# First maxima ahead of VectorE's tables, weights ahead of the last stores, two banks for a pair: five small edits to a fused attention, expert and gated-product kernel

## The chip, the cores and the metric

One Trainium2 chip, one core. The metric is device microseconds of the whole kernel, the median of repeated runs. An engine's queue runs its instructions in the order in which they were issued, and the kernel's author sets that order. SyncE (SP) and ScalarE (ACT) issue transfers on queues of their own, GpSimd (POOL) on a third.

## The reference

```python
# 1. attention with 32 global tokens and a window: B=4, H=8, 512 local + 32 global rows, D=64
k_all, v_all = concatenate([k_g, k_l], axis=2), concatenate([v_g, v_l], axis=2)
out_g = matmul(sm(scale * matmul(q_g, k_all.T)), v_all)            # global rows see everything
s_ll = where(abs(i - j) <= 32, scale * matmul(q_l, k_l.T), -1e9)   # local rows see a band
a_l = sm(concatenate([scale * matmul(q_l, k_g.T), s_ll], axis=-1)) # and the global rows
out_l = matmul(a_l, v_all)
x = rows of concatenate([out_g, out_l], axis=2)                    # 2304 tokens x 512
# 2. top-1 mixture of 8 experts, tokens with x @ w_skip <= 0 pass through
e_idx = argmax(xc @ w_gate, axis=1); gate_w = softmax(xc @ w_gate)[e_idx]
y[e_idx == e] = gate_w * (maximum(xc[e_idx == e] @ w1[e], 0) @ w2[e])   # w1[e] 512 x 1024
out = x; out[do_compute] = xc + y
# 3. gated product
return ((out @ w_a) * (out @ w_b)) @ w_out                         # 512 x 1536, 1536 x 512
```

## The kernel before, in words

Three phases follow each other in one program, 0 to about 132 us, to about 276 us, and to the end.

**Attention.** It runs over 16 pairs of heads (`NPAIR`), four pairs to a batch. For a pair p, `emit_S` makes the scores in PSUM (L963, half a pair per call with k), `emit_M` adds the band mask and takes row maxima on VectorE (L975), `emit_E` does the exponentials on ScalarE (L986) and, on GpSimd, copies the columns of the global keys to a tile of their own (`smg`, L988). `emit_T` transposes both (L1000, L1010). `emit_PV` multiplies with the values (L1026 and L1035) into a PSUM tile `o` of two banks and copies it to `ot` on ScalarE (L1040). `emit_X` multiplies `ot` with a table `xi` (L1059), which holds an identity to turn the rows and the router's weights beside it, so that VectorE then reads both router scores `lg` (L1063) and tokens `xt` (L1073) from the same `o` banks. The pool `ps_o` of these banks is shared by consecutive pairs; the pool `ps_s` holds six single banks for scores and transposes. The two pairs at the end (`last_pairs`) are written out by hand; `NPAIR - 2` is the last but one.

Each pair is cut into four slots (slot = 4 x pair and up), and side work hangs on slot numbers: `ROUTES` (routing of a batch), `SCATTERS` (the slots at which GpSimd scatters the four 128-row tiles of a batch to the experts' regions `xs`, L1252), and `GSTEPS` (the global queries' passes). `ZEROS` says in which pair SP stores which of the 16 blocks of zero rows to `xs` (L927, from the tile `zrow`); the scatters wait until these have landed. All loads and stores of a pair are put in a list `pend` and issued by SP one after the other. `start()` builds the table `xi`, issues its loads, runs the first two pairs' scores, maxima and exponentials, and keeps TensorE busy with matmuls that compute nothing (`idle`, L1371).

**Experts.** `WORK` lists the pieces (expert, first tile, number of row tiles); each is worked off in four quarter steps. One step is 12 matmuls of the first layer (L243), transposes (L1502) and six of the second (L1516), with weights that SP loads as `raw` (`fetch`, L152), ScalarE rounds to `hi` (L171) and VectorE subtracts to `lo` (L181). `st.fetch(i)` issues the loads of step i, two of 512 KB. `st.store_last()` issues the four stores of the last batch's tokens (L1264, x2d<-xt); `load_rows(2)` loads rows of work 2 (L157), which wait for the scatters. A scatter of the finished rows (L1528) waits for the stores of the last batch.

**Gated product.** `Late` runs 18 row tiles through `w_a`, `w_b` (L527) and `w_out` (L557), with sums kept in DRAM. The last tile is added in two halves of 256 columns (L559), each stored by its own DMA (L560).

## Time and profile before

| | us |
|---|---|
| median of three runs | 697.33 |
| lowest, highest | 695.45, 699.65 |
| the profiled execution's own time | 698.71 |
| its span in the profile | 696.9 |

The span runs from the first to the last event that the profiler records on the core; the time of the execution is 1.8 us longer. The profile gives busy time per engine, windows with the granted TensorE clock (1.00 is full speed) and the DMA engines' share, a timeline with the idle time before each piece of work and what released it, and a chain of work followed back from the end. "issue" in brackets means that the profile shows nothing that the engine waited for. SPq and ACTq are rows of the instruction queues that issue transfers; a row's length there includes waiting.

### The profile page before, as it was taken

What the parts mean: (1) busy time and instruction counts of PE and PEld (TensorE: products, weight loads), DVE (VectorE), ACT (ScalarE), POOL (GpSimd) and SP (SyncE); (2) the same over time, 40 slices, a digit from 0 to 9 for tenths busy, and PEclk for the clock granted to TensorE, in tenths of its full rate; (3) what the DMA queues carried; (4) which work ended last, traced back from release to release, by engine and by line L of the source; (5) the groups of instructions that cost most, each with busy time, mean ns of one, the idle gap of its engine ahead of it and who ended that gap; (6) DMA issues with size and microseconds to landing.
All of it is one profiled execution on the core that took longest, in us unless ns stands there. A gap on an engine that the chain in (4) does not pass through costs nothing.

```text
span 696.9 us, 16731 instructions
## 1 busy us (share of the span) xinstructions
PE 674.1 (97%) x6329; PEld 604.6 (87%) x6329; DVE 490.6 (70%) x1278; ACT 397.0 (57%) x973; POOL 130.8 (19%) x213
## 2 busy tenths in 40 slices
PE   8898999989999999999999999999999999999996
PEld 5777887868998888879999999999999999999995
DVE  5667878986968999967975796856375656544444
ACT  5667778865857884567467554544454544443220
POOL 4002213130101210010111122312231232212000
PEclk9999999999999999999999999999999999999999
DMA  8898778799999936632785589996599679549853
GB/s 282 219 233 281 240 222 280 229 310 361 371 369 346 346 121 228 219 134 92 226 333 128 77 188 327 313 221 119 65 268 216 121 151 327 75 61 213 288 179 111
DMA packets 86141, 154.86 MB, mean 222 GB/s; under 512 B 8663, under 2 KB 40279, under 8 KB 84516
## 3 DMA queue, kind: packets, MB, share of 16 engines
q1 hardware_dynamic: 69236, 110.80, 49.1%
q0 software_dynamic: 15744, 42.87, 27.5%
q8 instruction: 52, 0.85, 0.5%
q14 instruction: 37, 0.30, 0.1%
q10 hardware_dynamic: 1072, 0.04, 0.1%
HBM read 105.95 MB, written 51.18 MB: 225 GB/s over the span
## 4 chain that ended last, share of the span: by engine, by line
PE 80%; ACT 3%; DMA 3%; DVE 3%; issue 1%; POOL 0%; SPq 0%; DVEq 0%; POOLq 0%
PE bank L527 32%; PE bank L557 19%; PE acc L1516 8%; PE ph L243 6%; PE bank L583 3%; DMA raw<-w 3%; PE ph L235 2%; PE o L1059 1%; PE sps L963 1%; PE bank L462 1%; PE pt L1502 1%; ACT sm L986 1%; PE o L1035 1%; PE tps L1000 1%; PE tp L204 1%
## 5 line engine op out<-in xcount | busy, mean ns | idle before, releaser
L527 PE MATMUL bank<-xh,w 128*128 128x256 f32 (+1 forms) x1232 | 251.4, 290 | 0.1
L527 PEld LDWEIGHTS bank<-xh,w 128*128 128x128 f32 x1232 | 200.5, 189 | 4.2 <-DVE tmp L649 0.4
L527 PE MATMUL bank<-xl,w 128*128 128x256 f32 (+1 forms) x616 | 178.4, 290 | 0.0
L557 PE MATMUL bank<-woh,g 128*128 128x512 f32 (+1 forms) x412 | 143.7, 392 | 1.2 <-ACT o L563 0.5
L527 PEld LDWEIGHTS bank<-xl,w 128*128 128x128 f32 x616 | 116.1, 188 | 4.2
L181 DVE TENSOR_TENSOR lo<-raw,hi 128x1024 fp32r<-128x1024 f32 x72 | 87.0, 1221 | 11.9 <-ACT hi L171 10.8
L557 PEld LDWEIGHTS bank<-woh,g 128*128 128x128 f32 x412 | 77.3, 188 | 15.6 <-ACT o L563 1.0
L557 PE MATMUL bank<-wol,g 128*128 128x512 f32 (+1 forms) x206 | 80.4, 390 | 0.0
L171 ACT ACTIVATE hi<-raw 128x1024 fp32r<-128x1024 f32 x72 | 75.4, 1054 | 7.8 <-PE acc L1516 4.4
L607 ACT ACTIVATE g<-tmp 128x256 fp32r<-128x256 f32 (+1 forms) x88 | 37.8, 431 | 69.7 <-DVE tmp L649 68.9
L564 POOL DMA_DIRECT2D out<-raw x48 | 39.1, 815 | 141.6 <-ACT raw L563 127.0
L639 DVE TENSOR_TENSOR tmp<-bank,tmp 128x256 f32<-128x256 f32 (+1 forms) x44 | 18.8, 440 | 58.5 <-PE bank L527 58.4
L563 ACT ACTIVATE raw<-bank 128x512 f32<-128x512 f32 x48 | 28.6, 595 | 51.6 <-PE bank L557 50.5
L986 ACT ACTIVATE sm<-sm,nm 128x160 f32<-128x160 f32 x128 | 52.9, 419 | 7.8 <-DVE nm L975 7.8
L564 POOL DMA_DIRECT2D out<-o x37 | 29.6, 801 | 139.2 <-ACT o L563 101.7
L607 ACT ACTIVATE tmp<-bank 128x256 f32<-128x256 f32 (+1 forms) x88 | 34.6, 400 | 25.7 <-PE bank L527 22.2
L649 DVE TENSOR_TENSOR tmp<-bank,tmp 128x256 f32<-128x256 f32 (+1 forms) x88 | 38.9, 442 | 11.7 <-PE bank L527 10.2
L557 PEld LDWEIGHTS bank<-wol,g 128*128 128x128 f32 x206 | 38.7, 188 | 4.6
L645 DVE TENSOR_TENSOR g<-tmp,g 128x256 fp32r<-128x256 f32 (+1 forms) x88 | 38.3, 437 | 3.1 <-ACT g L607 1.4
L563 ACT ACTIVATE o<-bank 128x512 f32<-128x512 f32 x37 | 21.9, 596 | 31.9 <-PE bank L557 29.9
L243 PE MATMUL ph<-hi,xh 128*128 128x256 f32 x132 | 40.0, 303 | 0.0
L243 PE MATMUL ph<-hi,xl 128*128 128x256 f32 x132 | 37.5, 284 | 0.0
(265 smaller groups left out, 1276.5 us busy)
## 6 DMA issues: line engine op xcount, KB each, us to landing
raw<-w SPq DMA_DIRECT2D x64, 512.0 KB
out<-raw POOLq DMA_DIRECT2D x48, 256.0 KB, 4.6
out<-o POOLq DMA_DIRECT2D x37, 256.0 KB, 4.5
raw<-qk SPq DMA_DIRECT2D x28, 272.0 KB
xr<-x2d SPq DMA_DIRECT2D x25, 256.0 KB
raw<-wa SPq DMA_DIRECT2D x12, 512.0 KB
raw<-wb SPq DMA_DIRECT2D x12, 512.0 KB
raw<-wo SPq DMA_DIRECT2D x12, 512.0 KB
```

The source lines that it names most:

```text
L171: nc.scalar.activation(hi, rv, AF.Copy)
L181: nc.vector.tensor_tensor(lo, rv, hi.bitcast(F32), ALU.subtract)
L243: nc.tensor.matmul(ph, lhsT=x[:, d, :], rhs=w[:, d, :], start=(z == 0), stop=(z == 11))
L527: self.nc.tensor.matmul(bank[:, 0:n], lhsT=w[:, k], rhs=x[:, xp, k], start=start and z == 0, stop=z == 5, skip_group_check=not start)
L557: nc.tensor.matmul(acc[:, c], lhsT=a, rhs=w[:, c], start=(j == 0 and z == 0), stop=(j == 1 and z == 2))
L563: nc.scalar.activation(o, acc, AF.Copy)
L564: i = nc.gpsimd.dma_start(dst, o, accum_op=ALU.add if g else ALU.bypass)
L607: cp = lambda o, i: nc.scalar.activation(o, i, AF.Copy)
L645: tt(g4[2 * j + 1][:, h], (u, p)[h][j], g4[2 * j].bitcast(F32)[:, h], ALU.subtract)
L649: tt(v, (b1, b2)[h][j][:, 0:n], v, ALU.mult)
L986: st_.exp = nc.scalar.activation(sm, sm, AF.Exp, bias=nm[:, hh, j:j + 1], scale=-1.0, accum_out=dens[p][:, k, j, hh:hh + 1]).ins
L1516: nc.tensor.matmul(acc, lhsT=a[:, j, c], rhs=w[:, j, :], start=(q == 0 and z == 0), stop=(q == NQ - 1 and z == 5))
```

## The change

Five edits. (1) In `start()`, the eight copies of `ident` into `xi` move from VectorE to ScalarE, behind its three DMA issues; the copies of `tokid` and `pb8` on VectorE move from before the attention to the end of `start()`; the second call of `idle` goes. (2) `ZEROS` spreads the zero rows over pairs 0, 1, 2, 3, 5 and 6 (4, 3, 2, 2, 3, 2 blocks, before 3, 4, 3, 4 and 2 in pairs 0, 1, 2, 3 and 5), the first batch's scatters move from slots 24, 26, 28, 30 to 28, 29, 31, 33, and one pass of the global queries from slot 49 to 51. (3) For the last pair but one, `o` is two single banks of `ps_s` instead of one tile of `ps_o`; the copies and products that read it are done bank by bank. (4) `st.fetch(7)` is called ahead of `st.store_last()`. (5) The last half of the last output tile is stored from ScalarE's queue instead of SP's.

```diff
@@ -32,13 +32,13 @@
 
 ROUTES = (18, 34, 50)
 
-SCATTERS = ((24, 26, 28, 30), (35, 39, 43, 47), (51, 51, 53, 53))
+SCATTERS = ((28, 29, 31, 33), (35, 39, 43, 47), (51, 51, 53, 53))
 
 REUSE = 2
 
 LEAD = 38
 
-ZEROS = {0: (0, 3), 1: (3, 7), 2: (7, 10), 3: (10, 14), 5: (14, 16)}
+ZEROS = {0: (0, 4), 1: (4, 7), 2: (7, 9), 3: (9, 11), 5: (11, 14), 6: (14, 16)}
 
 WORK = [(0, 0, 1), (1, 0, 1), (1, 1, 1), (3, 0, 1), (2, 0, 2), (0, 1, 1), (4, 0, 1), (5, 0, 1), (6, 0, 1), (7, 0, 1)]
 
@@ -53,7 +53,7 @@
 WRAW, RAW2 = 6, 3
 
 GSTEPS = {(0, 0): (3, 5, 6), (0, 1): (8, 13, 14), (1, 0): (16, 21, 22), (1, 1): (24, 29, 30),
-          (2, 0): (32, 37, 38), (2, 1): (40, 45, 46), (3, 0): (43, 49, 54), (3, 1): (48, 53, 57)}
+          (2, 0): (32, 37, 38), (2, 1): (40, 45, 46), (3, 0): (43, 51, 54), (3, 1): (48, 53, 57)}
 
 
 
@@ -557,7 +557,7 @@
                         nc.tensor.matmul(acc[:, c], lhsT=a, rhs=w[:, c], start=(j == 0 and z == 0), stop=(j == 1 and z == 2))
                 if g == self.NM // 2 - 1:
                     nc.vector.tensor_tensor(o[:, c], acc[:, c], o[:, c], ALU.add)
-                    nc.sync.dma_start(dst[:, c], o[:, c])
+                    (nc.scalar if c.start else nc.sync).dma_start(dst[:, c], o[:, c])
             if g < self.NM // 2 - 1:
                 o = self.o[n % len(self.o)]
                 nc.scalar.activation(o, acc, AF.Copy)
@@ -939,9 +939,6 @@
         for b in range(B):
             nc.gpsimd.iota(tokid[32 * b:32 * b + 32, NT - 1:NT], pattern=[[0, 1]], base=b * (SL + SG), channel_multiplier=1)
 
-        nc.vector.tensor_copy(xg[:, 513:514].bitcast(I32), tokid[:, 16:17])
-        nc.vector.tensor_copy(base, pb8)
-
 
         sms = [c1.tile([128, 2, 2, 2, 160], F32, name=f"sm{k}") for k in range(2)]
         smg = [c1.tile([128, 2, 2, 2, SG], F32, name=f"smg{k}") for k in range(2)]
@@ -1016,14 +1013,19 @@
 
         def emit_PV(p):
 
-            o = oxs[p] = ps_o.tile([128, 2, 512], F32, tag="o", name="o")
+            if p == NPAIR - 2:
+                both, o = None, [ps_s.tile([128, 512], F32, tag="s", name="o2") for k in range(2)]
+            else:
+                both = ps_o.tile([128, 2, 512], F32, tag="o", name="o")
+                o = [both[:, k] for k in range(2)]
+            oxs[p] = both, o
             vt = vts[p]
             for j in range(2):
                 for k in range(2):
                     r = slice(64 * k, 64 * k + 64)
                     for hh in range(2):
                         c = slice(64 * hh, 64 * hh + 64)
-                        mm = nc.tensor.matmul(o[c, k, 128 * j:128 * j + 128], lhsT=vt[r, WIN, c], rhs=pts[p, 2][r, j, :],
+                        mm = nc.tensor.matmul(o[k][c, 128 * j:128 * j + 128], lhsT=vt[r, WIN, c], rhs=pts[p, 2][r, j, :],
                                               start=(j == 0), stop=False, skip_group_check=True)
             tick(mm)
             for i in range(4):
@@ -1032,12 +1034,17 @@
                     c = slice(64 * w, 64 * w + 64)
                     for hh in range(2):
                         r = slice(64 * hh, 64 * hh + 64)
-                        mm = nc.tensor.matmul(o[r, k, 128 * j + 64 * w:128 * j + 64 * w + 64], lhsT=vt[:, 2 * i + w, r],
+                        mm = nc.tensor.matmul(o[k][r, 128 * j + 64 * w:128 * j + 64 * w + 64], lhsT=vt[:, 2 * i + w, r],
                                               rhs=pts[p, hh][:, i, c], start=False, stop=True, skip_group_check=True)
                 if i % 2:
                     tick(mm)
             ot = ots[p] = ot_p.tile([128, 2, 2, 128], F32, tag="ot", name="ot")
-            st_.ot = nc.scalar.activation(ot.rearrange("p k j q -> p k (j q)"), o[:, :, 0:256], AF.Copy).ins
+            of = ot.rearrange("p k j q -> p k (j q)")
+            if both is None:
+                for k in range(2):
+                    st_.ot = nc.scalar.activation(of[:, k], o[k][:, 0:256], AF.Copy).ins
+            else:
+                st_.ot = nc.scalar.activation(of, both[:, :, 0:256], AF.Copy).ins
 
         xt, lg, lgp = {}, {}, {}
 
@@ -1053,15 +1060,17 @@
                 xt[b] = x_p.tile([128, 4, ROW], F32, tag="xt", name="xt")
                 lg[b] = r_p.tile([128, 4, 6, 9], F32, tag="lg", name="lg")
                 lgp[b] = r_p.tile([128, 4, 3, 9], F32, tag="lgp", name="lgp")
-            o, ot = oxs.pop(p), ots.pop(p)
+            (both, o), ot = oxs.pop(p), ots.pop(p)
             for k in range(2):
                 for j in range(2):
-                    mm = nc.tensor.matmul(o[:, k, 146 * j:146 * j + 146], lhsT=ot[:, k, j, :], rhs=xi[:, hp, :], start=True, stop=True)
+                    mm = nc.tensor.matmul(o[k][:, 146 * j:146 * j + 146], lhsT=ot[:, k, j, :], rhs=xi[:, hp, :], start=True, stop=True)
             tick(mm)
-            xp = o[:, :, 0:292].rearrange("p k (j h c) -> p k j h c", j=2, h=2)
+            parts = [(slice(0, 2), both[:, :, 0:292])] if both is not None else [(slice(k, k + 1), o[k][:, None, 0:292]) for k in range(2)]
+            xps = [(k, x.rearrange("p k (j h c) -> p k j h c", j=2, h=2)) for k, x in parts]
             ld = lg[b][:, :, 2 * hp:2 * hp + 2, :] if hp < 3 else lgp[b][:, :, 1:3, :]
-            nc.vector.tensor_tensor(ld.rearrange("p (k j) h e -> p k j h e", k=2), xp[:, :, :, :, 64:73],
-                                    dens[p][:, :, :, :, None].to_broadcast([128, 2, 2, 2, 9]), ALU.mult)
+            for k, xp in xps:
+                nc.vector.tensor_tensor(ld.rearrange("p (k j) h e -> p k j h e", k=2)[:, k], xp[:, :, :, :, 64:73],
+                                        dens[p][:, k, :, :, None].to_broadcast([128, k.stop - k.start, 2, 2, 9]), ALU.mult)
             if hp == 1:
                 nc.gpsimd.tensor_copy(xt[b][:, :, 513].bitcast(I32), tokid[:, 4 * b:4 * b + 4])
 
@@ -1070,10 +1079,10 @@
                     nc.vector.tensor_reduce(lgp[b][:, :, 0, :], lg[b].rearrange("p t h e -> p t e h"), AX.X, ALU.add)
 
             def tokens():
-                nc.vector.tensor_tensor(
-                    xt[b][:, :, 128 * hp:128 * hp + 128].rearrange("p (k j) (h d) -> p k j h d", k=2, h=2),
-                    xp[:, :, :, :, 0:64],
-                    dens[p][:, :, :, :, None].to_broadcast([128, 2, 2, 2, 64]), ALU.mult)
+                xv = xt[b][:, :, 128 * hp:128 * hp + 128].rearrange("p (k j) (h d) -> p k j h d", k=2, h=2)
+                for k, xp in xps:
+                    nc.vector.tensor_tensor(xv[:, k], xp[:, :, :, :, 0:64],
+                                            dens[p][:, k, :, :, None].to_broadcast([128, k.stop - k.start, 2, 2, 64]), ALU.mult)
                 sums()
 
             return tokens
@@ -1373,15 +1382,15 @@
         def start():
             nc.vector.memset(xi[0:64, :, 73:146], 0.0)
             nc.vector.memset(xi[64:128, :, 0:73], 0.0)
-            for hp in range(4):
-                nc.vector.tensor_copy(xi[0:64, hp, 0:64], ident[0:64, 0:64])
-                nc.vector.tensor_copy(xi[64:128, hp, 73:137], ident[64:128, 64:128])
             for s in range(2):
                 nc.scalar.dma_start(
                     xi[64 * s:64 * s + 64, :, 73 * s + 64:73 * s + 73],
                     w9[:, 64 * s:64 * s + 64, :].rearrange("a p e -> p a e"),
                 )
             nc.scalar.dma_start(w9s, w9.rearrange("a p e -> p a e"))
+            for hp in range(4):
+                nc.scalar.activation(xi[0:64, hp, 0:64], ident[0:64, 0:64], AF.Copy)
+                nc.scalar.activation(xi[64:128, hp, 73:137], ident[64:128, 64:128], AF.Copy)
             for g in gpts:
                 nc.gpsimd.memset(g[:, 4], 0.0)
             for k in range(2):
@@ -1396,9 +1405,10 @@
             emit_S(1)
             emit_M(1, 0)
             emit_E(1, 0)
-            idle(4)
             emit_T(0)
             emit_M(1, 1)
+            nc.vector.tensor_copy(xg[:, 513:514].bitcast(I32), tokid[:, 16:17])
+            nc.vector.tensor_copy(base, pb8)
 
         with tc.manual_schedule():
             start()
@@ -1604,8 +1614,8 @@
 
         for i in range(4, 7):
             st.fetch(i, (1,) if i < 6 else (0, 1))
+        st.fetch(7)
         st.store_last()
-        st.fetch(7)
         load_rows(2)
         for i, (k, q) in enumerate(steps):
             if i == NQ + 1:
```

## Rows read from the trace of the kernel before

**Rows 1.** The page, first part: busy time of each engine, its share, instructions.

```profile
PE 674.1 (97%) x6329; PEld 604.6 (87%) x6329; DVE 490.6 (70%) x1278; ACT 397.0 (57%) x973; POOL 130.8 (19%) x213
```

**Rows 2.** Windows by stage: length; busy us (count) of PE, PEld, DVE, ACT, POOL; clock; DMA; GB/s.

```profile
20.00:60.00 40.00, 35.60 (x853) 30.48 (x853) 27.84 (x156) 27.45 (x108) 3.06 (x11) 1.00 1.00 258
60.00:120.00 60.00, 57.56 (x1396) 49.15 (x1395) 48.91 (x275) 47.25 (x180) 15.69 (x29) 1.00 0.77 246
...
150.00:160.00 10.00, 6.74 (x36) 5.67 (x35) 5.62 (x10) 3.43 (x6) 1.31 (x1) 0.83 0.80 247
160.00:272.00 112.00, 112.00 (x740) 100.14 (x740) 96.32 (x125) 82.72 (x129) 15.23 (x11) 1.00 0.89 303
```

**Rows 3.** Timeline of the start: begin, length, engine, instruction [idle before <-releaser].

```profile
3.09 0.40 ACTq L1384 DMA_DIRECT2D w9s<-w  x1
...
7.15 0.15 DVE L942 COPY xg<-tokid 128x1 int32<-128x1 int32 x1 [5.94 <-POOL tokid L940]
...
8.09 0.19 DVE L1377 COPY xi<-ident 64x64 f32<-64x64 f32 x1
...
9.73 0.33 DVE L975 CUSTOM_DVE_ANT_0 sm<-sps,masks 128x160 f32<-128x160 f32 x1
...
10.10 0.43 ACT L986 ACTIVATE sm<-sm,nm 128x160 f32<-128x160 f32 x1 [7.80 <-DVE nm L975]
...
10.36 1.35 PE L963 MATMUL sps<-raw 64*64 64x128 f32 x32 [1.09 <-DVE nm L975]
...
14.28 1.54 PE L963 MATMUL sps<-raw 64*64 64x128 f32 x64
```

**Rows 4.** Windows of two short stretches of the start.

```profile
10.00:11.00 1.00, 0.58 (x6) 0.34 (x10) 1.00 (x11) 0.90 (x5) 0.00 (x0) 1.00 1.02 374
...
18.00:21.00 3.00, 3.00 (x49) 2.60 (x47) 1.65 (x5) 2.58 (x10) 0.00 (x0) 1.00 0.12 38
```

**Rows 5.** Timeline of TensorE around 33 us.

```profile
33.26 0.65 PE L1026 MATMUL o<-ptg,vt 64*64 64x128 f32 x10 [1.72 <-issue]
```

**Rows 6.** Timeline of GpSimd and TensorE at the first scatter.

```profile
65.47 1.23 POOL L1252 DMA_INDIRECT xs<-xt,slu  x1 [2.15 <-PE o L1035]
...
67.07 0.44 PE L1010 MATMUL tpg<-ident,smg 128*128 128x128 f32 x2 [0.57 <-POOL smg L988]
```

**Rows 7.** Timeline of TensorE and GpSimd in the last two pairs.

```profile
122.74 0.67 PE L1026 MATMUL o<-ptg,vt 64*64 64x128 f32 x16 [1.20 <-DVE xt L1073]
...
125.60 0.29 POOL L988 COPY smg<-sm 128x128 f32<-128x128 f32 x1 [1.70 <-ACT sm L986]
```

**Rows 8.** The chain that ended last, around 141 us: begin, length, what.

```profile
140.91 11.69 DMA raw<-w
```

**Rows 9.** Timeline of SyncE's queue, ScalarE and TensorE, 136 to 165 us.

```profile
136.35 3.52 SPq L1264 DMA_DIRECT2D x2d<-xt  x4
...
148.22 1.05 ACT L171 ACTIVATE hi<-raw 128x1024 fp32r<-128x1024 f32 x1
152.63 1.06 ACT L171 ACTIVATE hi<-raw 128x1024 fp32r<-128x1024 f32 x1 [3.35 <-DMA raw<-w]
...
154.01 0.44 PE L1502 MATMUL pt<-ident,hr 128*128 128x128 f32 x2 [3.26 <-ACT hr L247]
...
164.33 1.05 ACT L171 ACTIVATE hi<-raw 128x1024 fp32r<-128x1024 f32 x1
```

**Rows 10.** Windows of two short stretches around the first expert steps.

```profile
136.00:141.00 5.00, 4.74 (x30) 3.93 (x29) 4.30 (x16) 3.09 (x7) 3.12 (x2) 1.00 1.05 352
...
155.00:158.60 3.60, 3.60 (x14) 3.05 (x13) 2.59 (x3) 1.20 (x2) 0.00 (x0) 0.53 0.94 251
```

**Rows 11.** Timeline of VectorE and SyncE's queue at the end.

```profile
690.15 0.42 DVE L559 TENSOR_TENSOR raw<-bank,raw 128x256 f32<-128x256 f32 x1 [0.25 <-PE bank L557]
...
689.93 1.57 SPq L560 DMA_DIRECT2D out<-raw  x1
...
691.55 0.42 SPq L560 DMA_DIRECT2D out<-raw  x1
```

## Prediction

> **What bounds the kernel now.** The first line of the page comes first: TensorE is busy for 674.1 us of a span of 696.9 [rows 1]. That leaves 22.8 us in which it does nothing, so a change that leaves the matmuls alone can win only from these, from matmuls that compute nothing (the line L1371), and from matmuls run at the lower clock. The table of windows by stage says where these are: 4.40 us idle in 20 to 60 us, 2.44 in 60 to 120, 3.26 in the ten microseconds after 150, none from 160 to 272 [rows 2]. The same table has the DMA share: 1.00 in 20 to 60, where nothing can be asked of the queues, and 0.77 in the next sixty. Then the timeline of the start, engine by engine, for who is late first; the waits of TensorE; the chain of what ended last; and the timeline of the tail.
>
> **Start.** VectorE's first row maximum runs at 9.73, although its scores were made early. In front of it stand the copy of tokid, which waited 5.94 us for GpSimd, a copy of base, two memsets, and eight copies of ident of 0.19 (one of the eight is shown) [rows 3]. ScalarE waited 7.80 for that maximum. TensorE waited 1.09 at 10.36 because the score bank of the second pair had not been emptied, then ran four L1371 matmuls, which the change drops, and began the third pair's scores at 14.28.
> After the change VectorE has only the memsets before the maxima, which wait for scores instead, near 6. The eight copies go to ScalarE. They have no row there; bounds: 0.19 each as on VectorE, or 0.43, what the larger exponential takes, so 1.5 to 3.4 us. ScalarE's last DMA issue ends at 3.49, so they end between 5.0 and 6.9. I take 0.24, nearer the small copy: they end at 5.4, ahead of the first exponential at about 6.2; at the upper bound 0.7 is lost. What is late next is the keys: moved ahead, TensorE meets the loads of the second and third pair, which are still arriving (374 GB/s in 10 to 11, share 1.02) [rows 4]. Of the 3.6 us by which the maxima move I therefore give the third pair's scores 2.0 (14.28 to 12.3), with 1.0 and 2.5 as bounds. The shift lives on only if the queues let it, and they do: in 18 to 21 their share is 0.12 [rows 4], since the next load waits for TensorE. **-2.0.** The two moved copies (0.15 for the first) fall behind the second pair's maxima, where no exponential waits for VectorE.
>
> **Zero rows and scatters.** In 20 to 60 us TensorE's waits are mostly "issue": 1.7 us in one place, at 33.26, in the middle of a group of sixteen matmuls that use the same tiles [rows 5]. The wait has no releaser in the profile. In the stage after it, where the queues have room, TensorE idles at 37% of the rate, so I lay part of the 4.40 us at the door of the full queues. The zero rows (16 stores of L927) spread later: by the end of pair 3 eleven are issued instead of fourteen, and two go to pair 6, where the share is 0.77. Bounds: nothing (the waits have another cause), or the idle time of 20 to 60 comes down to the rate of 60 to 120, 4.40 - 40 x 2.44/60 = 2.8. I take **-1.0**, under half, as only three of sixteen leave the crowded pairs. The first scatter waited 2.15 and then held GpSimd, so that GpSimd's copy smg came late and TensorE waited 0.57 [rows 6]. From slot 24 to 28 that goes: **-0.5** (0 to -0.6). GSTEPS moves one group's pass two slots, among ScalarE work that has no gap there: 0, at most 0.5 either way.
>
> **Banks of the last pair but one.** TensorE waits 1.20 at 122.74 for VectorE to empty the o banks [rows 7]; with two banks of its own it need not. But what is late next is ScalarE: GpSimd's copy for the last pair waited 1.70 for an exponential and ran at 125.60, and the transpose behind it can't come earlier. TensorE would do its work sooner and wait there. **-0.2**; from 0 to -1.2, the whole wait. The extra halves are one ScalarE and two to three VectorE instructions, with slack on both.
>
> **Weights ahead of the last stores.** In the chain, "DMA raw<-w" holds 11.69 us from 140.91 [rows 8]: from the issue of step 7's weights to their landing. ScalarE waited 3.35 for it (split at 152.63) and TensorE 3.26, until 154.01 [rows 9]. SP had issued four stores before it, from 136.35 on. They are 4 x 256 KB = 1.05 MB, and the queues moved 352 GB/s [rows 10], so they put 3.0 us of traffic ahead. With the two calls exchanged the weights are issued near 136.4, 4.5 us sooner. The landing moves by 3.0 (only bytes count) to 4.5 (issue counts), to 149.6 at worst, and ScalarE is free for it at 149.27, the end of the split before it [rows 9]. The wait of 3.26 shrinks to some 0.4: -2.8.
> [...] The gap of 1.72 at 33.26 was followed by no fall: the stage's clock is 1.00 [rows 2]. With 0.4 of gap I expect none. Less 0.1 for what ScalarE loses elsewhere, **-4.4**; bounds: -1.5 (half of the wait stays, and with it the low clock), and 3.26 + 1.7 = -4.96.
> The stores go out 1 to 4 us later. Behind them are the scatter of finished rows and the row loads of work 2, which wait for POOL's scatters anyway. What is late next is step 8: its split ran at 164.33 [rows 9] and would be wanted near 160, and its weights are issued no sooner than before, as the row loads ahead of them don't move. The share is 0.94 in 155 to 158.6. That is the second rival.
>
> **Tail.** The last add ends at 690.57. SP's issue of the first half runs from 689.93 to 691.50, that of the second from 691.55 to 691.97 [rows 11]. On ScalarE's queue the second half can go at 690.6 and, at 0.40 for an issue as at 3.09 [rows 3], is out by 691.0. The end then hangs on the first half's 691.50: **-0.4** (0 to -1.0).
>
> **Sum.** -2.0 - 1.0 - 0.5 - 0.2 - 4.4 - 0.4 = -8.5. The profiled execution took 698.71 around its span of 696.9; it becomes 690.2. It lies 1.38 above the median of 697.33, which becomes **688.8**.
>
> **Rivals.**
> 1. *Step 8 is late instead.* With TensorE 4 to 7 us ahead, step 8's weights and work 2's rows arrive where they did, and 2 to 3 us of the gain comes back as waits of ScalarE behind 158. For it: shares of 0.94 before 158.6; against it: no wait at all in 160 to 272. 688.8 + 2.5 = 691.3. Chance 0.20.
> 2. *The exchange doesn't do what it says.* The weights land as late as before because others take their share of the queues. For it: the four stores and the weights' own 1.05 MB are 2.1 MB, 6.0 us at 352 GB/s, and the landing took 11.69, so half of that time went to something else. Against it: what of this was issued between 136.4 and 140.91 falls behind the weights too. 688.8 + 4.4 = 693.2. Chance 0.10.
> 3. *The attention gives nothing.* With the share at 1.00 in 20 to 60, what start and zero rows win is waited for there. 688.8 + 3.5 = 692.3. Chance 0.10.
> 4. *Slower.* If TensorE, being ahead, idles before each single-tile step behind 154 as long as it did before 154.01, each of the eight steps there costs 1.7 at the low clock; from five on, 8.5 us, it eats the whole sum. All eight: 697.3 - 8.5 + 4.4 + 8 x 1.7 = 706.8. Against it: TensorE has no gap in 160 to 272. Chance 0.03.
> 5. *The clock falls at the start.* Without the four L1371 matmuls TensorE idles instead, and the clock goes to the lower level for as long as it did after 154: 688.8 + 1.7 = 690.5. Against it: it was 1.00 in 10 to 11, where TensorE was busy for 0.58 [rows 4]. Chance 0.04. [...]
>
> **How the numbers follow.** Forecast 0.53, the rivals 0.47 together. The likeliest case alone spans 686.3 to 691.0: the zero rows at 0 and at -2.8, the start at -1.0 and -2.5. The range reaches down 4.0, where zero rows (1.8 more), banks (1.0), tail (0.6) and start (0.5) go well together, to 684.8, and up to rival 2's 693.2 and a little, 693.4. Outside are rival 4 and two rivals at once, on the upper side some 0.12. About 0.5% (3.5 us) is what a measurement of this kernel can tell from no change, so faster means under 693.8: 0.87; within, 0.09, two of the rivals 1 to 3 together; slower, 0.04, rival 4 and the unforeseen.
>
> **What would show it.** The first maximum near 6 and the third pair's scores near 12.3; no row over 1 us of "issue" in 20 to 60; the wait at 122.74 gone with the last pair's transpose hardly earlier; "DMA raw<-w" in the chain under 4 us of hold on TensorE around 150, and no stretch at 0.53 behind it; two last stores on two queues. I am wrong if TensorE's idle time comes back between 155 and 190, if scores of pairs 1 to 3 wait for "DMA raw<-qk" for more than 2 us, or if the clock falls elsewhere.

## The result: slower, and the profile after

The changed kernel takes 702.35 us against 697.31, a ratio of 1.0058 (95% interval 1.0029 to 1.0086), about 4 us: slower by 0.6%, where 688.8 and faster were forecast. Its profiled execution took 704.41, its span is 702.2.

The windows of the changed kernel, same stretches and columns as [rows 2], and one more, 180 to 190:

```profile
20.00:60.00 40.00, 35.56 (x829) 30.96 (x828) 27.40 (x153) 26.48 (x102) 2.75 (x10) 0.96 0.85 245
60.00:120.00 60.00, 53.50 (x1221) 45.64 (x1220) 42.96 (x244) 40.53 (x159) 12.57 (x24) 0.94 0.73 222
150.00:160.00 10.00, 10.00 (x66) 8.58 (x64) 9.80 (x18) 7.22 (x13) 1.59 (x2) 1.00 0.80 297
160.00:272.00 112.00, 109.17 (x709) 96.92 (x709) 92.78 (x119) 81.12 (x126) 16.20 (x11) 0.98 0.91 310
180.00:190.00 10.00, 7.17 (x42) 5.72 (x41) 8.56 (x10) 6.79 (x11) 2.05 (x1) 0.92 1.07 373
```

The kernel before, 180 to 190:

```profile
180.00:190.00 10.00, 10.00 (x71) 9.00 (x70) 9.79 (x14) 8.99 (x15) 2.05 (x1) 1.00 1.07 370
```

Four things are to be seen. 20 to 60 idles as before (4.44 us for 4.40), although the queues are less full (0.85 for 1.00). 60 to 120, which had 2.44 us idle, has 6.50, and its clock is 0.94. The gap behind 150 is gone, with its low clock. A gap of 2.83 stands at 180 to 190, where there was none at the same share of the queues (1.07).

How far the changed kernel is ahead or behind follows from when the same work begins in the two timelines (the values of a pair are L1026, now L1028; each expert step has one group of second-layer matmuls):

| work | before | after | difference |
|---|---|---|---|
| values of pair 0 | 15.95 | 12.70 | -3.25 |
| values of pair 1 | 23.29 | 21.70 | -1.59 |
| values of pair 2 | 31.11 | 33.16 | +2.05 |
| values of pair 3 | 39.32 | 39.23 | -0.09 |
| values of pair 7 | 70.60 | 68.64 | -1.96 |
| values of pair 8 | 77.64 | 80.27 | +2.63 |
| values of pair 10 | 92.62 | 98.41 | +5.79 |
| values of pair 15 | 128.50 | 134.26 | +5.76 |
| second layer of the first step | 138.03 | 144.09 | +6.06 |
| of the seventh step | 160.65 | 161.83 | +1.18 |
| the one behind the turning of work 4's rows | 183.49 | 188.19 | +4.70 |
| two steps further | 191.10 | 197.30 | +6.20 |
| end of the span | 696.9 | 702.2 | +5.3 |

The start wins some 2 us and has lost them by pair 3: at 12.70 only one of the sixteen matmuls of pair 0's values ran, the other fifteen came at 13.91, 2.04 us ahead; and at pair 2 the kernel before still has its stall of 1.72 in front of it [rows 5]. Pairs 7 to 10 lose 7.75. The exchange wins 4.9, and 5.0 are lost again behind 180. The end wins 0.9.

Timeline of the start, on VectorE, ScalarE and TensorE:

```profile
5.56 0.33 DVE L972 CUSTOM_DVE_ANT_0 sm<-sps,masks 128x160 f32<-128x160 f32 x1 [3.65 <-PE sps L960]
...
5.38 0.25 ACT L1393 ACTIVATE xi<-ident 64x64 f32<-64x64 f32 x1
5.92 0.43 ACT L983 ACTIVATE sm<-sm,nm 128x160 f32<-128x160 f32 x1 [0.29 <-DVE nm L972]
...
11.34 1.54 PE L960 MATMUL sps<-raw 64*64 64x128 f32 x55 [0.25 <-DMA raw<-qk]
...
13.91 0.66 PE L1028 MATMUL o<-ptg,vt 64*64 64x128 f32 x15 [0.86 <-issue]
...
26.69 0.27 PE L1136 MATMUL gop<-vt,gpt 128*32 128x64 f32 x2 [2.55 <-issue]
```

The first maximum runs at 5.56, when its scores are there, a copy on ScalarE takes 0.25, and the third pair's scores begin at 11.34 instead of 14.28. But at 26.69 TensorE stands for 2.55 us between matmuls of one group, and "issue" names nothing. Behind it, in 28 to 31.8, the granted clock is 0.55.

The last zero rows ahead of the first scatter on SyncE's queue, in the kernel before and in the changed one:

```profile
58.48 1.63 SPq L927 DMA_DIRECT2D xs<-zrow  x2
```

```profile
65.42 0.86 SPq L927 DMA_DIRECT2D xs<-zrow  x2
```

Timeline of pairs 7 and 9 in the changed kernel, on GpSimd, VectorE and TensorE:

```profile
73.31 1.23 POOL L1261 DMA_INDIRECT xs<-xt,slu  x1 [5.04 <-DMA vt<-v]
74.52 0.34 POOL L985 COPY smg<-sm 128x128 f32<-128x128 f32 x1
...
74.91 0.44 PE L1007 MATMUL tpg<-ident,smg 128*128 128x128 f32 x2 [2.62 <-POOL smg L985]
...
88.90 0.69 DVE L1084 TENSOR_TENSOR xt<-o,den 128x512 f32<-128x512 f32 x1 [3.81 <-DMA x2d<-xt]
...
89.70 1.13 PE L1028 MATMUL o<-ptg,vt 64*64 64x128 f32 x16 [2.97 <-issue]
```

The first scatter still stands, now 5.04 us instead of 2.15 [rows 6], with smg and TensorE behind it. GpSimd was ready for it 4.84 us after the issue of the last zero rows before (65.47 - 2.15 - 58.48), and 2.85 us after it now (73.31 - 5.04 - 65.42); it went 7.0 and 7.9 us after that issue. Later VectorE waits 3.81 before it writes tokens, and TensorE cannot have the o banks until it has: 88.90 + 0.69 = 89.59, then 89.70. The transfers that the profile names are those that landed last and need not be what the instruction waits for; the experiments tell that apart.

Chain of waits and timeline at 180 to 190, SyncE's queue and TensorE:

```profile
177.14 2.13 SPq L157 DMA_DIRECT2D xr<-xs  x2
```

```profile
178.93 8.80 DMA xr<-xs
```

```profile
187.07 1.36 PE L204 MATMUL tp<-ident,xr 128*128 128x128 f32 x8 [2.00 <-DMA xr<-xs]
```

The rows of work 4 are issued at 177.14, behind seven steps of weights (14 loads), and take 8.80 us to land, while the share of the queues is 1.07.

Timeline of the last pair and of the tail:

```profile
132.03 0.44 PE L1007 MATMUL tpg<-ident,smg 128*128 128x128 f32 x2
...
696.48 0.38 SPq L560 DMA_DIRECT2D out<-raw  x1
...
696.69 0.42 DVE L559 TENSOR_TENSOR raw<-bank,raw 128x256 f32<-128x256 f32 x1 [0.26 <-PE bank L557]
...
697.15 0.37 ACTq L560 DMA_DIRECT2D out<-raw  x1
```

From the last add's end to the span's end it is 702.2 - 697.11 = 5.1 us; it was 696.9 - 690.57 = 6.3 [rows 11]. This pair of profiles shows more than the rest: in all the profiles below and these two it is 5.1 to 6.4 with two queues (eleven profiles, mean 5.8) and 6.1 to 6.6 with one (nine, mean 6.3), so 0.5.

### The profile page after: what moved, and what is told of

Same layout as the page of the kernel before. It is cut to its first block, busy times and chain, and to the rows that moved or that the text cites. A ratio compares the mean times of both kernels' runs of the same rounds, so it can differ in the third digit from the quotient of the medians.

```text
span 702.2 us, 16730 instructions
## 1 busy us (share of the span) xinstructions
PE 677.2 (96%) x6325; PEld 607.8 (87%) x6325; DVE 489.2 (70%) x1272; ACT 399.1 (57%) x982; POOL 131.2 (19%) x213
## 4 chain that ended last, share of the span: by engine, by line
PE 74%; issue 4%; ACT 4%; DMA 3%; DVE 3%; SPq 0%; POOL 0%; POOLq 0%; DVEq 0%; ACTq 0%
PE bank L527 32%; PE bank L557 19%; PE acc L1526 6%; PE ph L243 4%; PE bank L583 3%; PE ph L235 2%; DMA xr<-xs 1%; ACT sm L983 1%; PE o L1066 1%; PE bank L462 1%; PE sps L960 1%; PE gps L1109 1%; PE o L1037 1%; DMA xr<-x2d 1%; DMA x2d<-tmp,xr 1%
## 5 line engine op out<-in xcount | busy, mean ns | idle before, releaser
L243 PE MATMUL ph<-lo,xh 128*128 128x256 f32 x132 | 37.4, 283 | 0.0
```

The source lines that it names most:

```text
L243: nc.tensor.matmul(ph, lhsT=x[:, d, :], rhs=w[:, d, :], start=(z == 0), stop=(z == 11))
```

## The experiments

Every ratio is against the kernel before on the same chip. The kernel before took 697.3 us in the first comparison and 705.9, 706.2, 707.0, 699.8 and 707.1 in the five sets below, so only ratios are compared.

### First set: which edit costs

**The exchange alone**, `st.fetch(7)` ahead of `st.store_last()` in the kernel before.

> The kernel before with the two calls exchanged alone (step 7's weights ahead of the last stores). Theory P, the prediction's: the gap of 3.26 us before 154.01 and the stretch at 0.53 behind it go for good, 697.3 - 4.4 = 692.9. Theory S (stream): from the landing of the last scatter on, SyncE's queue sets the stage, and it is not moved by the exchange; the profile of the changed kernel gained 4.9 us by step 8 and lost 5.0 us at 178.9 to 187.7 waiting for the rows of work 4. By S the gap at 154 goes, a gap of some 3 us comes at about 173 to 183 in front of the transposes of work 4's rows, with the low clock behind it, and the time is 697.3 within 0.7.

Measured: 1.0002 (0.9972 to 1.0033). Its windows and TensorE's wait:

```profile
150.00:160.00 10.00, 10.00 (x69) 8.72 (x68) 9.88 (x15) 8.36 (x15) 3.45 (x4) 1.00 0.96 358
...
180.00:190.00 10.00, 8.16 (x54) 6.90 (x54) 9.28 (x12) 7.90 (x13) 2.05 (x1) 1.00 1.07 372
```

```profile
188.24 1.38 PE L204 MATMUL tp<-ident,xr 128*128 128x128 f32 x8 [1.77 <-DMA xr<-xs]
```

Theory S fits: the gap leaves 154 and stands before work 4's rows, without any delay of the attention by the other edits. But on some chips it stands there without the exchange too: the run with the banks alone, below, has 0.47 us at 145.58 and 1.71 at 188.32. No profile of the kernel before was taken on this chip, so the 1.0002 alone does not say that 4.4 us were won and lost again.

**The exchange, and work 4's rows ahead of the weights.**

```diff
             if i == NQ + 1:
                 load_rows(3)
+                load_rows(4)
...
-                if q == 0 and k + 2 < len(WORK):
+                if q == 0 and 4 < k + 2 < len(WORK):
```

> The kernel before with the exchange, and the loads of work 4's two row tiles issued right behind work 3's, ahead of seven steps of weights instead of behind them. Theory P: the rows were never late without the attention's delay, so this is as the exchange alone, 692.9. Theory S: the wait moves off the rows, and the 4.9 us are kept as far as the weights of the next steps come in time: 692.4 if they do, up to 695 if each of them is late in turn.

Measured: 1.0007 (0.998 to 1.0034). Timeline of ScalarE and TensorE:

```profile
171.56 1.06 ACT L171 ACTIVATE hi<-raw 128x1024 fp32r<-128x1024 f32 x1 [2.91 <-DMA raw<-w]
...
172.94 0.99 PE L1516 MATMUL acc<-hi,hh 128*128 128x512 f32 x2 [1.72 <-ACT hh L1503]
```

The rows are in time, and the weights behind them are late by as much. Theory S, with its worse bound: whatever is put first, something is late.

**New ZEROS and SCATTERS alone**, in the kernel before.

> The kernel before with the new ZEROS and SCATTERS alone. Theory P: 697.3 - 1.5 = 695.8. Theory Z: the zero rows and the first scatter moved by one pair each, so the scatter still stands behind the zero rows and holds GpSimd (the copy smg behind it, and TensorE behind that, 2.6 us), and the last tile's scatter, now in the pair that writes the token buffer again, holds VectorE's tokens (TensorE 3.0 us), with the low clock behind both: 7.8 us lost from pair 7 to pair 10, of which up to 4 come back in pairs 2 to 7 from queues with fewer zero rows. So 701.1, with 699 to 705 as bounds. Theory T (start): the attention's loss comes from the pairs that start sooner and meet the loads; then this is 697.3 or less.

Measured: 1.0063 (1.0031 to 1.0094), +4.4 us. TensorE waits 0.72 for smg at 74.10, and at pair 9:

```profile
89.26 0.67 PE L1026 MATMUL o<-ptg,vt 64*64 64x128 f32 x16 [3.62 <-issue]
```

697.3 + 4.4 = 701.7, and theory Z said 701.1; theory T falls.

**The changed kernel with the ZEROS and SCATTERS of before.**

> The changed kernel with the ZEROS and SCATTERS of before. Theory Z: waits for smg and for tokens in pairs 7 to 10 go; the start's 3.25 us stay; the exchange gives nothing: 702.35 - 7.8 = 694.5, or up to 697 if the queues eat a part of the start's gain. Theory T: 702 as the changed kernel. Theory P: 697.3 - 7.0 = 690.3.

Measured: 0.9936 (0.9911 to 0.996), 692.8 on the scale of 697.3; the two long waits of pairs 7 to 9 are gone. Theory Z, though the time lies below its 694.5 to 697; the third set shows that on such a chip the move of GSTEPS gives 3.2 us, which the theory left out.

### Second set: holds, stream, start, banks

**Step 8's weights ahead of the row loads**, ZEROS and SCATTERS of before.

```diff
         st.fetch(7)
         st.store_last()
+        some(6)
+        st.fetch(8)
         load_rows(2)
```

> The changed kernel with the ZEROS and SCATTERS of before, and step 8's weights (1.05 MB) issued behind the last stores but ahead of the row loads that wait for the scatters; since these weights belong to an expert chosen by rank, the six small VectorE instructions that rank the experts run ahead of the expert loop too. The same kernel without this last edit had a ratio of 0.9936 to before. Theory S: SyncE's stream behind the last scatter sets the stage to 190 us, so 1.05 MB that go out in the 9 us in which SyncE waits shorten it by 2.8 us at 370 GB/s, the wait for the rows of work 4 (1.78 us) goes, and the low clock behind it (1 to 1.7 us): ratio 0.988 to 0.990. Rival: the stage is bound by ScalarE's and VectorE's splits, not by the stream: 0.9936 as without it, or above, since VectorE's six instructions (some 1.2 us) stand in front of its splits.

Measured: 0.9959 (0.993 to 0.9988), no better than without. The wait for work 4's rows is gone, and TensorE waits for VectorE:

```profile
160.49 1.22 PE L1526 MATMUL acc<-hi,hl 128*128 128x512 f32 x2 [2.22 <-DVE hl L1514]
```

So the rival holds for this edit; the next set tries the ranking in pieces.

**ZEROS of before, new SCATTERS**, in the changed kernel.

> The changed kernel with the ZEROS of before and the new SCATTERS. The zero rows have then landed long before slot 28, so the scatter does not hold GpSimd behind them; but the last tile of batch 0 is still scattered in slot 33, in the pair that writes its token buffer again. Theory Z says that both holds cost: the wait for smg goes (2.6 us and the low clock behind it), the wait of 3.0 us before TensorE's values in pair 9 stays: between the two neighbours, 0.9936 + 0.005 = 0.9986. If the zero rows alone are the cost: 0.994. If the reuse of the buffer alone is: 1.0058.

Measured: 1.000 (0.997 to 1.0031). Timeline of GpSimd, VectorE and TensorE:

```profile
71.08 1.23 POOL L1261 DMA_INDIRECT xs<-xt,slu  x1 [0.97 <-PE gtp L1122]
...
89.22 0.69 DVE L1084 TENSOR_TENSOR xt<-o,den 128x512 f32<-128x512 f32 x1 [4.54 <-DMA raw<-qk]
...
90.01 0.80 PE L1028 MATMUL o<-ptg,vt 64*64 64x128 f32 x12 [3.70 <-issue]
```

With the zero rows in time GpSimd is held 0.97 us, for 5.04 in the changed kernel; the later scatters alone cost 0.64% against the version with both old (0.9936, measured on another chip). The profile names a load of q and k for VectorE's wait here and a store above; the third set takes the scatter out of the way.

**The start alone**, and **the banks alone**, in the kernel before.

> The kernel before with the start's edits alone (copies to ScalarE, two copies later, four dummy matmuls dropped). By the profile of the changed kernel the first values' matmuls come 3.25 us sooner (12.70 instead of 15.95). If the shift lives on as the prediction has it: ratio 0.9955 (3.1 us; the prediction's own term is 2.0, 0.997). If the loads and the full queues in 20 to 60 us take it back: 1.000.

> The kernel before with two banks of their own for the last pair but one, alone. The prediction: 0.2 us, ratio 0.9997, since ScalarE is late next; the whole wait of 1.2 us: 0.998. In the profile the wait at 122.74 goes either way; by the prediction the last pair's transposes (126.05) move by less than 0.3 us against the values of the pair before.

Measured: 0.9988 (0.9963 to 1.0013) and 1.001 (0.9982 to 1.0039). In the start's run pair 0's values began at 13.34, 2.63 us ahead of the banks' run on the same chip (15.97). TensorE then stood 2.28 us at 26.27, in the same group as in the changed kernel, and pair 2's values began level (31.13 for 31.03); but the banks' run stood 1.45 us in the middle of these, and at pair 3 the start's run is 1.48 ahead (37.49 for 38.97), at pair 15 1.49 (134.54 for 136.03). So part of the shift lives on in this pair of profiles, and neither edit's time can be told from nothing.

### Third set: the changed kernel again, and better versions

**The changed kernel itself**, and **GSTEPS alone** (`(3, 0): (43, 49, 54)` to `(43, 51, 54)` in the kernel before).

> The changed kernel itself, beside the other three on one chip. If the loss of the first comparison belongs to the kernel: ratio 1.0058 again (1.003 to 1.009). If it belongs to the chip on which it was taken: 1.000 or less.

> The kernel before with the pass of the global queries moved from slot 49 to 51, alone. The prediction: 1.000 (0.5 us either way). In the profiles of the second chip the values of pair 11 and those of pair 15 lie 31.2 to 33.8 us apart in the four kernels without this move and 29.2 to 29.5 in the three with all edits, since TensorE creeps through its values and global products at slots 50 and 51, a matmul or two at a time with 0.4 to 0.5 of "issue" between. Theory G: the move is the cause, 3 us: ratio 0.9955. If the banks and the start are: 1.000.

Measured: 0.9998 (0.9967 to 1.0028) and 0.9954 (0.9925 to 0.9983). In the first two sets TensorE creeps through pair 13 in all five kernels with the order of before; here in the kernel with the exchange alone, three of six such rows:

```profile
121.57 0.25 PE L1035 MATMUL o<-pt,vt 128*64 128x64 f32 x1 [0.49 <-issue]
122.30 0.34 PE L1035 MATMUL o<-pt,vt 128*64 128x64 f32 x3 [0.47 <-issue]
123.05 0.28 PE L1127 MATMUL gop<-vt,gpt 128*32 128x64 f32 x2 [0.41 <-issue]
```

On the third set's chip the moved pass saves 3.2 us. In the first comparison's profile of the kernel before there is no such creeping, and from pair 11's values to pair 15's it is 27.19 us before and 27.15 after: the move is worth nothing there. That can account for the difference between 1.0058 and 0.9998, as far as it is above the intervals. The terms measured alone add up to both: start -0.8, zero rows and scatters +4.4, tail -0.5, the rest nothing, +3.1 for the +4 of the first comparison; with -3.2 for GSTEPS -0.1, for the -0.1 here.

**Scatters in slots 28, 29, 30, 31** instead of 28, 29, 31, 33, with the ZEROS of before, in the changed kernel.

> The changed kernel with the ZEROS of before and the first batch's scatters in slots 28, 29, 30, 31: the same late first scatter as the changed kernel, but the last one two slots ahead of the pair that writes its token buffer again. With slot 33 (and the same ZEROS) TensorE waited 3.70 us in pair 9 and the ratio was 1.000. Theory Z (reuse of the buffer): that wait goes, and the time is that with the old SCATTERS, 0.9936 (0.991 to 0.996). If something else in the late scatters costs: 1.000.

Measured: 0.9915 (0.9885 to 0.9946), the fastest version; beside the changed kernel on the same chip it is 0.83% or 5.9 us less. The windows of 60 to 100, the changed kernel of the first comparison first (on this chip it was busy 33.25, at the same clock):

```profile
60.00:100.00 40.00, 34.41 (x824) 30.12 (x823) 26.93 (x151) 24.48 (x96) 9.16 (x17) 0.91 0.64 193
```

```profile
60.00:100.00 40.00, 38.37 (x905) 32.24 (x899) 31.37 (x171) 28.62 (x111) 9.36 (x18) 1.00 0.69 214
```

Against the run with slot 33 the third scatter stands one slot earlier and the fourth two, and TensorE has no wait over 0.4 in 60 to 100. That is the reuse of the token buffer: the pool has two, batch 2 writes the one of batch 0 from pair 8 on, and slot 33 lies in pair 8.

**The ranking in pieces**, two instructions in each of the first three steps, step 8's weights and the row loads behind them; ZEROS and SCATTERS of before.

> The changed kernel with the ZEROS and SCATTERS of before; the six VectorE instructions that rank the experts run two by two in the first three expert steps instead of later, and step 8's weights are issued ahead of the row loads that wait for the scatters. Put in one lump ahead of the loop these edits took the wait for the rows of work 4 away, but TensorE then waited 0.92 and 2.22 us for VectorE's halves, ratio 0.9959. Theory S (stream): without the lump the stage from the first second-layer matmul to the row wait's end shortens by 2.8 us and the low clock behind the wait goes: 0.9936 - 0.005 = 0.989. Rival: VectorE's and ScalarE's splits set the stage as soon as the stream doesn't: 0.993 to 0.996.

Measured: 0.9922 (0.9895 to 0.9948), within the interval of the version without it. The wait is 2.23 us at 161.84, for the rows of the next work. 0.9922 lies between 0.989 and the rival's range, and the interval takes in part of the rival's; what is late is not the splits, though, but the rows that now stand behind the weights.

### Fourth and fifth set: zero rows, creeping, exchange

**The third batch's scatters later** (slots 54, 54, 55, 55), in the kernel before.

> The kernel before with the four scatters of the third batch in slots 54, 54, 55, 55 instead of 51, 51, 53, 53; the pass of the global queries stays in slot 49. In the second set of runs TensorE crept through slots 50 and 51 of this order, a matmul or two and then 0.4 to 0.5 of "issue" over some 5 us, and moving the pass to slot 51 gave 0.9954. Theory C: GpSimd's scatters beside the many small matmuls are the cause; then the creeping goes or moves to slots 54 and 55, and the ratio is 0.995 to 0.998. Theory D: it is the place in TensorE's program (its instructions arriving late), whatever GpSimd does: the creeping stays at the values of pair 13 and the ratio is 1.000.

Measured: 1.0094 (1.0059 to 1.0128). Inconclusive: on this chip the kernel did not creep there (5.87 us between the values of pairs 13 and 14, as in the first comparison), and the later scatters make the last row loads late (TensorE waits 2.13 for them at 133.23).

**New ZEROS with the SCATTERS of before**, in the changed kernel.

> The changed kernel with the SCATTERS of before and the new ZEROS. The first scatter, in slot 24, then stands behind zero rows that are issued in the same pair: GpSimd is held for most of a pair, the copies smg behind it wait, and TensorE waits 2.6 us or more for smg around 66 to 73. The last scatter is two to three slots ahead of the reuse of its buffer. Theory Z, both holds cost alike: between the changed kernel and the one with both old, 0.994 to 1.000, with the wait for smg at 2.6 us or more. If only the reuse of the buffer costs: 0.9925.

Measured: 1.0099 (1.0066 to 1.0131), outside both expectations. TensorE's waits in 60 to 100 us (total, times, longest):

```profile
PE tpg L1007 <- POOL smg L985: 7.2, 2, 4.6
```

GpSimd is held twice, 5.72 us before the first scatter and 6.48 before the third: the hold behind the zero rows is larger with earlier scatters, and there is no wait at pair 9. The zero rows moved by a pair, and the scatter has to move by more than that.

**No zero rows in pairs 0 to 2**, in the kernel before, a single execution whose time is not compared.

```diff
-ZEROS = {0: (0, 3), 1: (3, 7), 2: (7, 10), 3: (10, 14), 5: (14, 16)}
+ZEROS = {3: (0, 4), 5: (4, 8), 6: (8, 12), 7: (12, 16)}
-SCATTERS = ((24, 26, 28, 30), (35, 39, 43, 47), (51, 51, 53, 53))
+SCATTERS = ((34, 34, 34, 34), (35, 39, 43, 47), (51, 51, 53, 53))
```

> The kernel before with no zero rows in pairs 0 to 2 (four each in pairs 3, 5, 6, 7) and the first batch's scatters all in slot 34; for the place of TensorE's waits of "issue" alone, as the late scatters cost time of their own. The prediction laid 1.0 us of the idle time in 20 to 60 us at the zero rows' door. If the zero rows cause the stalls in the middle of groups of matmuls, there is none over 0.6 us between 15 and 38 us (every run so far had one of 0.7 to 2.6 there). If they are independent of the zero rows, the one near 33 us (1.45 to 2.0 in the runs with the start of before) is there as it was.

Its window of 20 to 60, and VectorE and TensorE at pair 9:

```profile
20.00:60.00 40.00, 39.49 (x1008) 34.62 (x1009) 32.49 (x181) 32.03 (x127) 3.46 (x13) 1.00 0.74 228
```

```profile
88.14 0.69 DVE L1073 TENSOR_TENSOR xt<-o,den 128x512 f32<-128x512 f32 x1 [7.41 <-DMA xs<-xt,slu]
...
88.94 1.13 PE L1026 MATMUL o<-ptg,vt 64*64 64x128 f32 x16 [6.37 <-issue]
```

Without zero rows in the first pairs TensorE has no gap over 0.3 us between 15 and 60. In this run, then, the stalls of "issue" there went with the zero rows, nearly all 4.4 us of them; the four blocks of pair 3, which stayed, made none. Stalls come back at 67.53 (1.02) and 74.65 (1.87), beside the zero rows of pairs 5 to 7. The late scatters cost 6.37 at pair 9, and here the profile names the scatter (xs<-xt,slu) as what VectorE's write of the tokens waited for.

**The fastest version without the exchange.**

> The fastest version so far (the changed kernel with the ZEROS of before and the first scatters in slots 28 to 31, ratio 0.9915) with the last stores ahead of step 7's weights again. Theory S (stream): the exchange moves the gap from 154 to 187 and gives nothing: 0.9915 (0.989 to 0.994). Theory P: 4.4 us are lost, 0.998.

Measured: 0.9978 (0.9946 to 1.001), on a chip without the creeping, where the move of GSTEPS gives nothing: 0.9915 + 0.0046 = 0.9961 is what the version with the exchange would have there by sum. The number alone does not settle it; its windows do:

```profile
150.00:160.00 10.00, 7.66 (x39) 6.98 (x39) 4.75 (x9) 3.56 (x7) 1.15 (x1) 0.66 0.86 274
180.00:190.00 10.00, 10.00 (x74) 9.22 (x73) 9.77 (x12) 8.57 (x14) 1.73 (x1) 1.00 1.07 371
```

One gap, at 152 without the exchange, before work 4's rows with it (1.85 at 186.81, in the run with it on the third set's chip).

**Zero rows in pairs 2, 3, 5, 6**, and **in pairs 1, 2, 3, 5, 6**, scatters in slots 30, 30, 31, 31.

> The changed kernel with zero rows in pairs 2, 3, 5 and 6 (four each, none in pairs 0 and 1) and the first batch's scatters in slots 30, 30, 31, 31. With none in pairs 0 to 2, TensorE had been busy 39.49 of 40 us from 20 to 60, and its stalls of "issue" were gone; with the zero rows of before and scatters in slots 28 to 31, it was 33.6 to 34.9 busy. Theory ZR (zero rows stall TensorE's instructions in the first pairs): stalls over 0.6 us before 38 us go, 2 to 4 us are won against that version, ratio 0.986 to 0.988 on a chip where that one has 0.9915, 0.992 to 0.994 on one where it has 0.9978. Rival: the stalls move with the zero rows into pairs 5 and 6, or GpSimd is held behind the last of them around slot 30 and the copy smg is late: no better than that version.

> As the kernel beside it, with zero rows in pairs 1, 2, 3, 5 and 6 (2, 3, 4, 4, 3). Theory ZR: with half as many in pairs 1 and 2 one stall near 33 us stays, some 1 us: between the kernel beside it and the version with the zero rows of before (0.9915 or 0.9978 by chip). Rival: fewer in pair 6 frees the scatters earlier, and this one is the faster of the two.

Measured: 0.9927 (0.9896 to 0.9958) and 0.9967 (0.9938 to 0.9996), no better than 0.9915. Timelines of TensorE, two rows of the first and one of the second:

```profile
25.29 0.27 PE L1136 MATMUL gop<-vt,gpt 128*32 128x64 f32 x2 [1.18 <-issue]
...
72.22 0.42 PE L1136 MATMUL gop<-vt,gpt 128*32 128x64 f32 x14 [3.39 <-issue]
```

```profile
76.11 0.65 PE L1136 MATMUL gop<-vt,gpt 128*32 128x64 f32 x14 [3.51 <-issue]
```

The rival: stalls of 3.39 and 3.51 stand behind the zero rows of pair 6 (issued from 63.32 and 66.44), where the fastest version, with the zero rows of before, has none over 0.4 in 60 to 100, and GpSimd is held 7.66 and 6.27 us before the first scatter. Theory ZR's sign fails too: the first kernel has 1.18 at 25.29, although its first zero rows are issued at 31.95 and the share of the queues is 0.06 in 24 to 25. So there are such stalls without zero rows as well. The second has 4.95 at 50.73, behind pair 3's four blocks, as many as before; the fastest version has 3.04 at 54.17 in the same group, so this one did not move.

## Why the prediction was wrong

The sign that it named for itself came: TensorE's idle time came back between 155 and 190 (2.83 us in 180 to 190). But the larger part of the miss lies in the attention.

- **Zero rows and scatters: the step that failed.** -1.5 was predicted; alone they cost +4.4 (1.0063), and in the changed kernel 5.9 against the zero rows of before with the scatters in slots 28 to 31. "From slot 24 to 28 that goes" took the scatter four slots later, and left out that two zero-row blocks also move one pair, four slots, later (pair 5 to 6). In slots the distance stayed, in time it shrank from 4.84 to 2.85 us, and the hold grew from 2.15 to 5.04 us. And of the last tile's scatter, now in slot 33, the prediction asked only what waits behind it on GpSimd, not who needs its source: the token buffer is written again in pair 8. No rival had either mechanism; rival 3 let the attention's gain vanish, not turn into a loss. The low clock behind the two gaps adds to them (0.91 in 60 to 100).
- **The price of the zero rows, -1.0, was right in kind only.** Most of the "issue" stalls go with them (39.49 of 40 busy without them in the first three pairs). But the term said that fewer in the crowded pairs give back part; in the changed kernel 20 to 60 idles 4.44 for 4.40, and stalls of 3.4 to 3.5 us stand behind the zero rows that were moved to pair 6. That a stall of 1.18 stands with no zero rows ahead of it shows that they are not the only cause.
- **Weights ahead of the last stores: -4.4 predicted, 0 measured alone (1.0002).** The gap and the low clock behind it went as worked out (4.9 us by the seventh step's second layer). The 1.7 us that the term's sum, and rivals 4 and 5, charge for the low clock are the 3.6 us at 0.53 in 155 to 158.6 [rows 10], 3.6 x 0.47; in the changed kernel the clock there is 1.00, and it has 0.55 in 28 to 31.8 behind its gap of 2.55 us and 0.66 in 187 to 192 behind that of 2.00. The failed half-sentence is that only step 8 need be looked at; rival 1 ("the second rival" in that term's own words) had the mechanism, SyncE's stream standing where it did, at 2 to 3 us and 0.20. It took all 5.0 in the changed kernel, at work 4's rows. On a chip of the first comparison's kind the exchange was not measured by itself; the fastest version without it is at 0.9978 for a sum of 0.9961, within the interval. A stage without any wait of TensorE in 160 to 272 [rows 2] was read as one with slack; with the share at 1.07 it had been just in time.
- **Start: -2.0 predicted, -0.8 measured alone (0.9988).** Maxima (5.56) and copies (0.25 for the 0.24 taken) came as worked out, the third pair's scores 2.94 us sooner, beyond the bound of 2.5, and the values 2.04. What failed is "the shift lives on": a stall of 2.3 to 2.6 us between pair 1 and pair 2 took part of it in the run alone and, with the clock at 0.55 behind it, all of it in the changed kernel. Rival 5 did not happen: the clock is 1.00 up to 20 us, and its fall at 28 comes behind that stall.
- **Banks, -0.2:** not to be told from nothing (1.001), as said. The wait at 122.74 is gone, and the last pair comes no earlier against the pair before it: 134.26 - 127.56 = 6.70 for 5.76.
- **GSTEPS, 0:** right in the first comparison's profiles, -3.2 us alone on another chip; in the first two sets the order of before made TensorE creep, with 0.41 to 0.49 us of "issue" at a time in the rows above.
- **Tail, -0.4:** right, 0.5 by the mean of all profiles; that the first pair of profiles shows 0.9 to 1.2 is chance.
- **The range's sums:** by the terms named, the likeliest case spans 686.5 to 690.8, not 686.3 to 691.0, and the reach downward is 3.9, not 4.0. Nothing hangs on it: the measured time lies 9 us above the range.

What stays open: what makes the stall that no zero rows precede; why some chips show the creeping in pair 13, and what in it the place of the pass decides; the run meant for it fell on a chip without it.

## What to carry to other kernels

When a wait and what it waits for are both moved, look at their distance: here it shrank from 4.84 to 2.85 us, and the hold grew from 2.15 to 5.04. A transfer moved later has two ends, the engine that issues it and the next writer of its source: with the last scatter in slot 33 TensorE waited 3.70 us in pair 9, with it in slot 31 never over 0.4 in 60 to 100. A stage in which TensorE never waits is no proof of slack: with the gap of 3.26 us at 154 taken out, 2.83 us of idle time came in 180 to 190, where the DMA share is 1.07 with and without it, ahead of rows that took 8.80 us to land. Stalls inside a group of matmuls that share their tiles, put down to "issue", went here for the most part with the zero rows: in 20 to 60 TensorE was busy for 39.49 us without them in the first three pairs, for 35.60 in the kernel before.

## What the runs showed of the hardware

Behind stores of zero rows, 257 KB each, TensorE stopped for up to 4.95 us in the middle of a group of matmuls (at 50.73, with zero rows in pairs 1, 2, 3, 5 and 6); without them in the first three pairs it was busy for 39.49 us of 20 to 60, in the other runs for 32.7 to 37.3. The page of the changed kernel lists two queues of the kind "instruction", of which this one moves more:

```profile
q8 instruction: 52, 0.85, 0.5%
```

That is 0.85 MB in 52 packets, 16 KB each. The profile does not show who waits for them. That TensorE does, in its stalls of "issue", is the author's estimate.

The times of these packets in the traces speak for it. In the changed kernel they keep pace with TensorE between 157 and 199 us: 126 matmuls, each with its weight load, begin between the packets at 156.99 and 176.18, and 122 from there to the next one, at 198.97. Of the 57 stalls of "issue" of 0.6 us or more that TensorE has between 10 and 80 us in the twenty profiles, 40 end 1.2 to 1.8 us after a packet of q8 has ended; a moment taken at random lies there in 11% of cases. In the changed kernel a packet runs from 23.74 to 25.05, and TensorE goes on at 26.69. The stall without zero rows is of this kind too: its packet ended at 23.90, and TensorE went on at 25.29. That is shown by the times alone, and the other 17 stalls do not lie in that band.
